# A fused attention-plus-MLP block: the opening's transposes as a stream of their own, V in column halves, small zero products

## The chip, the cores and the metric

The kernel runs on one core of one Trainium2 chip. The time is that of one execution on the device, in microseconds; the time before is the median of 6 runs. The engines are TensorE (PE; its weight loads are PEld), VectorE (DVE), ScalarE (ACT), GpSimd (POOL) and SyncE (SP), which issues the DMAs.

## The reference

Inputs are bf16: tokens x of 2048 x 640, `wqkv` 640 x 1920, 32 small matrices `w_phi` of 20 x 20, `wo` 640 x 640, `w1` and `w3` 640 x 1536, `w2` 1536 x 640.

```python
xn = layernorm(x)                                   # over 640
q, k, v = split(xn @ wqkv)                          # 32 heads of 20
pq, pk = q @ w_phi, k @ w_phi                       # per head
phi_q = concat(softmax(pq), softmax(-pq))           # 40 features per head
phi_k = concat(softmax(pk), softmax(-pk))
kv, z = phi_k^T @ v, sum(phi_k)                     # over 2048 tokens
o = (phi_q @ kv) / (phi_q . z + 1e-6)
out = x + o @ wo + (silu(xn @ w1) * (xn @ w3)) @ w2
```

## The kernel before

There are 16 token tiles of 128 rows, and 4 blocks of 512 tokens. `x_tok` holds the tokens, `xnT` the normalised tokens transposed (640 features as 5 chunks of 128 partitions). PSUM has 8 banks; a step asks `banks(1)` or `banks(2)` for the bank or pair that comes free first.

The work is written as Python generators, *streams*, that yield steps; a step is a short function which issues a few instructions on any of the engines. A planner in the kernel's own Python puts the steps in order: it keeps a clock for each engine, gives each instruction a planned cost, and at every turn takes the step whose planned start is earliest; between equals, the stream with the lower number goes first. A step with TensorE work can't be planned to start before TensorE is free plus 0.15; a step without any that belongs to a stream in `URGENT` is taken ahead when its engine will reach it within 4 planned microseconds of TensorE's clock. MLP steps go last while VectorE's clock is more than `LAG` = 4.0 ahead of TensorE's. The order of each engine's queue is fixed by that when the program is built; on the chip the engines wait for each other by semaphores.

The streams before are, in order of number:

- `norms`: the first loads and constants (`first_loads`, `consts`), then for each tile the statistics (`ln_stats`: VectorE, and POOL for the reciprocal root) and the normalisation in place (`ln_apply`); then `block_diag` on POOL, the later tiles, and at the end `consts_late`, which writes `eps` and the column of ones of `v2` on POOL.
- `fold_k`: five steps that fold w_phi into the K weights, giving `Wkp`, from `wqkT`, which a DMA transposes.
- `attention`: zero products, the transposes and V of tiles 0 to 3, then K (`k_tile`, two exponentials on ACT into `ekt`) and V (`v_tile`) of the other tiles with the Q fold (`Wqp`), then the sum over tokens (`kv_sum`, `kv_store`), then Q (`q_proj`, `q_tok`).
- `k_norms`: the softmax sums of K on VectorE (`S64`, `rS64`) and the division on POOL.
- `loads`: for tiles 4 to 15 the DMA transposes of normalised tokens into `xnT`, with the rest of the weight loads between them on SP's queue.
- `o_transposes`, `mlps` (48 steps of 10 products of 512 columns, with a tanh on ACT and two operations on VectorE), and `outs` (the output products of each tile, after the MLP).

The first four tiles are transposed on TensorE: `xn_transpose` makes five transposes into a bank of PSUM, and `evac` copies the bank to `xnT` on ACT or VectorE, whichever is planned to be done first. `v_tile` makes ten products of 320 columns into two banks, and ACT copies them into `v2`. In `attention` the order of these steps is written out by hand:

```python
yield lambda: warm_up(10, True)
yield from transposed(0)
yield lambda: warm_up(4, False)
yield from transposed(1)
yield v(0)
yield from transposed(2)
yield v(1)
yield from transposed(3)
yield v(2)
yield v(3)
```

`transposed(t)` yields nothing until `ln_apply(t)` is planned. `warm_up(n, first)` clears 512 columns of the tile `t1` and multiplies them n times; nothing reads the result, in bank 7.

Of the kernel before, what the change touches and what calls it, by code (L numbers as in the profile page):

```python
# [3 lines left out]
ACT = mybir.ActivationFunctionType  # L4
# [7 lines left out]
DH = 20  # L12
F = 1536
T = S // 128
DC = D // 128
# [227 lines left out]
def bass_parallel_sum__linear_kernel_hedgehog__glu_gated_swiglu__prompt_kernel(  # L243
# [48 lines left out]
    xnT = new("xnT", [128, DC, S], bf)  # L292
# [14 lines left out]
    wv = new("wv", [128, DC, D], bf, RKV + 6400)  # L307
# [14 lines left out]
    v2 = new("v2", [128, T, H * 21], bf, RV)  # L322
# [16 lines left out]
    def bank(k, cols=512, off=0, rows=128):  # L339
        return PS[0:rows, k * 512 + off:k * 512 + off + cols]  # L340
# [5 lines left out]
    def mm(o, l, r, start, stop, shared=False, cost=None):  # L346
        n = free(r)
        P.op("PE", "matmul", [o], [l, r], (o, l, r),
             dict(start=start, stop=stop, skip_group_check=shared),
             cost=max(n / 2400 + 0.003, 0.055) if cost is None else cost)  # L350
# [5 lines left out]
    def free(ap):  # L356
        n = 1
        for s in ap.shape[1:]:
            n *= s
        return n  # L360

    def act(o, i, f, scale=1.0):
        P.op("ACT", "activation", [o], [i], (o, i, f), dict(scale=scale),
             cost=0.17 + free(o) / 1200)
# [21 lines left out]
    def memset(eng, o, v):  # L386
        P.op(eng, "memset", [o], [], (o, v), cost=0.15 + free(o) / 960)
# [18 lines left out]
    def load_x(a, b):  # L406
        P.dma("SP", x_tok[:, a:b, :], x_t[:, a:b, :])
# [53 lines left out]
            P.op("ACT", "activation", [o], [o, s, z], (o, o, ACT.Identity), dict(bias=z, scale=s),  # L461
                 cost=0.9)

    def warm_up(n, first):

        z = t1[:, 2, :]
        if first:
            memset("DVE", z, 0.0)
        for _ in range(n):
            mm(bank(7), z[:, 0:128], z, True, True)  # L470

    def xn_transpose(t, k):
        for dc in range(DC):
# [29 lines left out]
    def proj(t, w, k):  # L503
        for q in range(2):
            for i in range(DC):
                mm(bank(k + q, 320), xnT[:, i, t * 128:(t + 1) * 128],
                   w[:, i, 320 * q:320 * q + 320], i == 0, i == DC - 1)

    def v_tile(t, k):
        proj(t, wv, k)  # L510
# [158 lines left out]
    def banks(n):  # L669

        def free_at(k):
            return max([o.end for i in range(k, k + n) for o in P.bank.get(("P", i), {}).values()],
                       default=0.0)
        return min(range(0, 8, n), key=free_at)

    done = dict.fromkeys(("w", "ln", "t", "f", "k", "n", "kv", "q", "o", "h"), 0)

    def norms():
        yield lambda: (first_loads(), consts())
        for t in range(4):  # L680
            yield lambda t=t: ln_stats(t, 1)
            if t:
                yield lambda t=t: ln_apply(t - 1)
                done["ln"] = t
        yield lambda: ln_apply(3)
        done["ln"] = 4
        yield block_diag
        todo = []
        for t in range(4, T + 2, 2):
            if t == T or t > done["k"] + 8 or t == 12 and done["w"] < 8:  # L690
                for u in todo:
                    yield lambda u=u: ln_apply(u)
                    done["ln"] = u + 1
                todo = []
            if t == T:
                break
            while t > done["k"] + 8 or t == 12 and done["w"] < 8:
                yield None
            yield lambda t=t: ln_stats(t, 2)
            for u in todo:  # L700
                yield lambda u=u: ln_apply(u)
                done["ln"] = u + 1
            todo = [t, t + 1]
        yield consts_late

    def fold_k():
        for dc in range(DC):
            yield lambda dc=dc: fold_mm(1, dc, banks(2))
        done["f"] += 1
# [3 lines left out]
    def k_norms():  # L713
        for t in range(T):
            while done["k"] <= t:
                yield None
            yield lambda t=t: k_norm(t)
            done["n"] = t + 1

    def transposed(t):  # L720
        while done["ln"] <= t:
            yield None
        yield lambda: xn_transpose(t, banks(1))
        done["t"] = t + 1

    def loads():
        while done["t"] < 4:
            yield None
        for t in range(4, T):
            while done["ln"] <= t:  # L730
                yield None
            yield lambda t=t: P.dma("SP", xnT[:, :, t * 128:(t + 1) * 128], x_tok[:, t, :], True)
            done["t"] = t + 1
            if t == 7:
                yield lambda: (w13(512, 1024), load_x(12, 16))
                done["w"] = 8
            if t == 9:
                yield lambda: w13(1024, 1536)
                done["w"] = 12
                yield lambda: P.dma("SP", wqkT[:, 0:DC, :], A_wqkv[:, 0:D], True)  # L740
                done["f"] = 2

    def attention():
        def v(t):
            return lambda: v_tile(t, banks(2))

        yield lambda: warm_up(10, True)
        yield from transposed(0)
        yield lambda: warm_up(4, False)
        yield from transposed(1)  # L750
        yield v(0)
        yield from transposed(2)
        yield v(1)
        yield from transposed(3)
        yield v(2)
        yield v(3)
        while done["f"] < 1:
            yield None
        for t in range(T):
            while done["t"] <= t:  # L760
                yield None
            yield lambda t=t: k_tile(t, banks(2))
            done["k"] = t + 1
            if t >= 4:
                yield v(t)
            if 9 <= t < 14:
                while done["f"] < 2:
                    yield None
                yield lambda dc=t - 9: fold_mm(0, dc, banks(2))
        yield lambda: P.dma("SP", wo_s[:], A_wo.rearrange("(c p) d -> p c d", p=128))  # L770
        for fc in range(DC):
            yield lambda fc=fc: q_proj(0, fc, banks(1))
        while done["n"] < T:
            yield None
        yield lambda: memset("POOL", stg[:], 0.0)
        yield lambda: kv_sum((0, 1, 2, 3), banks(1))
        yield lambda: kv_sum((4, 5), banks(1))
        yield lambda: kv_store((0, 1, 2), banks(1))
        yield lambda: kv_store((3, 4), banks(1))
        done["kv"] = 1  # L780
        yield lambda: P.dma("SP", w2_s[:], B_w2.rearrange("(c p) d -> p c d", p=128))
        yield lambda: (load_xres(0), load_xres(1))
        for b in range(NB):
            for j in range(4):
                t = 4 * b + j
                yield lambda t=t: q_tok(t, 0)
                done["q"] = t + 1
                if b + 1 < NB:
                    for fc in range((5 * j + 3) // 4, (5 * j + 8) // 4):
                        yield lambda b=b, fc=fc: q_proj(b + 1, fc, banks(1))  # L790

    def o_transposes():
        for t in range(T):
            while done["q"] <= t:
                yield None
            yield lambda t=t: P.dma("SP", oT[:, :, t * 128:(t + 1) * 128], o_tok[:, t % 3, :], True)
            done["o"] = t + 1

    def mlps():
        for b in range(NB):  # L800
            for fc in range(FC):
                while done["t"] < 4 * b + 4 or done["w"] <= fc or b == 2 and done["t"] < T or b == 3 and not done["kv"]:
                    yield None
                yield lambda b=b, fc=fc: mlp(b, fc, banks(2))
            done["h"] = b + 1

    def outs():
        for t in range(T):
            while done["o"] <= t or done["h"] <= t // 4:
                yield None  # L810
            yield lambda t=t: out_tile(t, banks(2))

    MLPS = 6
    URGENT = {0: 4.0, 3: 4.0}
    streams = [norms(), fold_k(), attention(), k_norms(), loads(), o_transposes(), mlps(), outs()]
    n = len(streams)
    heads, alive = [None] * n, [True] * n
    while any(alive):
        best = None
        for i in range(n):  # L820
# [14 lines left out]
            if any(o.eng == "PE" for o in ops):  # L835
                at = max(P.ready(ops), P.free["PE"] + 0.15)
                if i == MLPS and P.free["DVE"] > P.free["PE"] + LAG:
                    rank = n
            else:
                at = P.start_of(ops[0])  # L840
                if i in URGENT:
                    now, mine = P.free["PE"], P.free[ops[0].eng]
                    if at <= max(now, mine) + 0.3 and at < now + URGENT[i]:
                        at = now + 0.1 - URGENT[i]
            if best is None or (round(at, 2), rank) < best[:2]:
# [3 lines left out]
        i, ops, after = best[2:]  # L849
# [65 lines left out]
```

The softmax here doesn't subtract the row's maximum and nothing guards it: scores larger than these inputs give would overflow.

## Time and profile before

| what | value |
|---|---|
| median of 6 runs | 277.71 us (277.48 to 278.0) |
| the profiled execution: time, span | 278.18 us, 276.5 us |
| TensorE busy | 268.9 us (97% of the span) |
| VectorE, ScalarE, GpSimd busy | 182.1, 106.3, 60.3 us |
| HBM read, written | 12.81 MB, 2.62 MB |
| TensorE clock granted, as recorded | 1.00 |

The span runs from the first to the last instruction. A row of a timeline has the start, the length, the engine, the line, the operation, what it writes and reads, and how many equal instructions it stands for; the idle time before it and what ended that stand in brackets. Nearly all instructions are recorded by one helper, so all rows show line 101, and one goes by the names of tiles. `PS` is PSUM, `t` is `t1`, `w_s` stands for the MLP's weights and `S`, `rS` for the softmax sums and their reciprocals. Matmuls are pipelined: a row's length includes the end of the last one, and the distance between the starts of rows is what one costs in a stream.

### The profile page before, as it was taken

What the parts mean: (1) busy time and instruction counts of PE and PEld (TensorE: products, weight loads), DVE (VectorE), ACT (ScalarE), POOL (GpSimd) and SP (SyncE); (2) the same over time, 40 slices, a digit from 0 to 9 for tenths busy, and PEclk for the clock granted to TensorE, in tenths of its full rate; (3) what the DMA queues carried; (4) which work ended last, traced back from release to release, by engine and by line L of the source; (5) the groups of instructions that cost most, each with busy time, mean ns of one, the idle gap of its engine ahead of it and who ended that gap; (6) DMA issues with size and microseconds to landing.
All of it is one profiled execution on the core that took longest, in us unless ns stands there. A gap on an engine that the chain in (4) does not pass through costs nothing.

```text
span 276.5 us, 4669 instructions
## 1 busy us (share of the span) xinstructions
PE 268.9 (97%) x1898; PEld 163.3 (59%) x1916; DVE 182.1 (66%) x319; ACT 106.3 (38%) x192; POOL 60.3 (22%) x93
## 2 busy tenths in 40 slices
PE   7899989999999999999999999999999999999996
PEld 2556666667448445555555555666446777777774
DVE  5459779898763897999899899978863111121212
ACT  2377978598922225444644545221220000000000
POOL 4415297899990100000000000000000000000000
PEclk9999999999999999999999999999999999999999
DMA  7971799630000810211111211322300222222211
GB/s 199 294 225 37 208 253 281 105 120 2 0 0 2 284 51 0 51 24 24 26 24 34 39 24 25 51 53 67 72 0 2 76 66 78 67 77 68 75 47 47
DMA packets 40326, 21.96 MB, mean 79 GB/s; under 512 B 26736, under 2 KB 40304, under 8 KB 40304
## 3 DMA queue, kind: packets, MB, share of 16 engines
q1 hardware_dynamic: 40304, 21.66, 30.9%
q8 instruction: 15, 0.25, 0.4%
q14 instruction: 7, 0.06, 0.1%
HBM read 12.81 MB, written 2.62 MB: 56 GB/s over the span
## 4 chain that ended last, share of the span: by engine, by line
PE 78%; DVE 6%; SPq 5%; DMA 5%; POOL 3%; issue 1%; ACT 0%; POOLq 0%; ACTq 0%
PE PS L101 78%; SPq L113 5%; DMA x_tok<-in_A_x_dram 5%; DVE bst L101 4%; POOL ekt L101 2%; POOL v L101 1%; DVE mv L101 1%; DVE S L101 1%; POOL eps L101 0%; ACT v L101 0%; DVE hT L101 0%; DVE t L101 0%; ACT Wqp L101 0%; DVE rS L101 0%; DVE xres L101 0%
## 5 line engine op out<-in xcount | busy, mean ns | idle before, releaser
L101 PE MATMUL PS<-xnT,w_s 128*128 128x512 bf16 x467 | 105.4, 379 | 0.7
L101 PEld LDWEIGHTS PS<-xnT,w_s 128*128 128x128 bf16 x480 | 46.7, 98 | 55.2 <-ACT Wkp L101 0.2
L101 PE MATMUL PS<-w_s,hT 128*128 128x320 bf16 (+2 forms) x384 | 54.9, 299 | 0.0
L101 DVE TENSOR_TENSOR xres<-PS,xres 128x640 bf16<-128x640 f32 (+2 forms) x17 | 13.3, 785 | 54.0 <-PE PS L101 54.0
L101 ACT ACTIVATE th<-PS 128x512 f32<-128x512 f32 x48 | 28.6, 599 | 46.0 <-PE PS L101 46.0
L101 PEld LDWEIGHTS PS<-w_s,hT 128*128 128x128 bf16 x384 | 37.6, 98 | 14.6
L101 DVE SCALAR_TENSOR_TENSOR t<-th,PS 128x512 bf16<-128x512 f32 x48 | 32.8, 683 | 16.6 <-ACT th L101 16.6
L101 POOL TENSOR_TENSOR ekt<-ekt,rS 128x640 bf16<-128x640 bf16 x32 | 39.5, 1277 | 4.1 <-DVE rS L101 4.1
L101 DVE SCALAR_TENSOR_TENSOR hT<-t,PS 128x512 bf16<-128x512 bf16 x48 | 33.0, 687 | 1.8 <-PE PS L101 0.2
L101 ACT ACTIVATE EqT<-PS 128x512 bf16<-128x512 f32 x40 | 21.7, 594 | 9.9 <-PE PS L101 9.9
L101 PE MATMUL PS<-Wkp,xnT 128*128 128x320 bf16 x160 | 23.9, 299 | 0.8 <-DMA xnT<-x_tok 0.7
L101 PE MATMUL PS<-wo_s,oT 128*128 128x320 bf16 (+2 forms) x160 | 24.5, 299 | 0.0
L101 DVE TENSOR_TENSOR prod<-PS,g_s 128x1280 bf16<-128x1280 f32 x16 | 23.9, 1491 | 0.6
L101 PE MATMUL PS<-wv,xnT 128*128 128x320 bf16 x160 | 24.2, 299 | 0.0
L101 ACT ACTIVATE ekt<-PS 128x640 bf16<-128x640 f32 x32 | 20.7, 719 | 6.1 <-PE PS L101 6.0
L101 DVE TENSOR_REDUCE S<-ekt 128x64 f32<-128x1280 bf16 x16 | 23.0, 1438 | 0.0
L101 PE MATMUL PS<-xnT,Wqp 128*128 128x512 bf16 x95 | 22.6, 379 | 0.3
L101 PEld LDWEIGHTS PS<-Wkp,xnT 128*128 128x128 bf16 x160 | 15.3, 98 | 7.2 <-ACT ekt L101 1.0
L101 PEld LDWEIGHTS PS<-wo_s,oT 128*128 128x128 bf16 x160 | 15.6, 98 | 6.1
L101 PEld LDWEIGHTS PS<-wv,xnT 128*128 128x128 bf16 x160 | 15.5, 98 | 5.9
L101 DVE BATCH_NORM_STATS2 bst<-x_tok 128x6 f32<-128x320 bf16 x32 | 15.3, 478 | 5.0 <-DMA x_tok<-in_A_x_dram 4.4
L101 ACT ACTIVATE e_s<-PS 128x64 f32<-128x64 f32 x32 | 9.0, 283 | 22.0 <-PE PS L101 21.0
(52 smaller groups left out, 161.0 us busy)
## 6 DMA issues: line engine op xcount, KB each, us to landing
w_s<-in_B_w_dram SPq DMA_DIRECT2D x6, 640.0 KB, 6.5
xres<-in_A_x_dram SPq DMA_DIRECT2D x16, 160.0 KB, 2.4
out_dram<-xres SPq DMA_DIRECT2D x15, 160.0 KB, 1.8
x_tok<-in_A_x_dram SPq DMA_DIRECT2D x3, 640.0 KB, 6.0
w_s<-in_B_w_dram SPq DMA_DIRECT2D x1, 1920.0 KB, 9.2
wv<-in_A_wqkv_dram SPq DMA_DIRECT2D x2, 400.0 KB, 4.7
wo_s<-in_A_wo_dram SPq DMA_DIRECT2D x1, 800.0 KB, 4.7
x_tok<-in_A_x_dram SPq DMA_DIRECT2D x4, 160.0 KB, 2.7
```

What stands on the lines that cost most here:

```text
L101: o = _Op(eng, lambda: m(*args, **kw), r, w, cost)
L113: o = _Op(eng, lambda: m(out, in_), self.regions(in_), self.regions(out), nbytes, True)
```

## The change

- The transposes of tiles 0 to 3 become a stream, `transposes`, which stands second, ahead of `fold_k`. So the planner decides where each goes. All later streams move up by one number, and `MLPS` and `URGENT` follow.
- V of tiles 0 to 3 is issued by column halves, `v_half(t, q)`: five products of 320 columns in one bank, and a copy of 320 columns on ACT. Each half is a step. Tiles 4 to 15 keep `v_tile`.
- The zero products before the first transposes are 7 of 512 columns instead of 10; then 10 rounds of 2 products of 88 columns, each over 64 of the 128 rows, and 8 rounds of 4 products of 66 columns, each over 32 rows. Products of one round write to different banks (0 to 3). The 4 zero products after tile 0 are gone.

```diff
-    def warm_up(n, first):
+    def warm_up():
 
         z = t1[:, 2, :]
-        if first:
-            memset("DVE", z, 0.0)
-        for _ in range(n):
+        memset("DVE", z, 0.0)
+        for _ in range(7):
             mm(bank(7), z[:, 0:128], z, True, True)
+        for n, cols, rep in ((2, 88, 10), (4, 66, 8)):
+            r = 128 // n
+            for _ in range(rep):
+                for i in range(n):
+                    mm(bank(i, cols), z[r * i:r * i + r, 0:128], z[r * i:r * i + r, 0:cols], True, True,
+                       cost=0.05 / n)
...
+    def v_half(t, q, k):
+        for i in range(DC):
+            mm(bank(k, 320), xnT[:, i, t * 128:(t + 1) * 128], wv[:, i, 320 * q:320 * q + 320],
+               i == 0, i == DC - 1)
+        act(v2[:, t, 336 * q:336 * q + 336].rearrange("p (h c) -> p h c", c=21)[:, :, 0:DH],
+            bank(k, 320).rearrange("p (h c) -> p h c", c=DH), ACT.Copy)
...
+    def transposes():
+        for t in range(4):
+            yield from transposed(t)
...
-        yield lambda: warm_up(10, True)
-        yield from transposed(0)
-        yield lambda: warm_up(4, False)
-        yield from transposed(1)
-        yield v(0)
-        yield from transposed(2)
-        yield v(1)
-        yield from transposed(3)
-        yield v(2)
-        yield v(3)
+        yield warm_up
+        for t in range(4):
+            while done["t"] <= t:
+                yield None
+            for q in range(2):
+                yield lambda t=t, q=q: v_half(t, q, banks(1))
...
-    MLPS = 6
-    URGENT = {0: 4.0, 3: 4.0}
-    streams = [norms(), fold_k(), attention(), k_norms(), loads(), o_transposes(), mlps(), outs()]
+    MLPS = 7
+    URGENT = {0: 4.0, 4: 4.0}
+    streams = [norms(), transposes(), fold_k(), attention(), k_norms(), loads(), o_transposes(), mlps(), outs()]
```

## The prediction

> **What bounds the kernel now.** The page first: TensorE is busy for nearly the whole span, and the chain that ended last is TensorE for 78%, the rest being a load and normalisation chain early on.
>
> ```profile
> PE 268.9 (97%) x1898; PEld 163.3 (59%) x1916; DVE 182.1 (66%) x319; ACT 106.3 (38%) x192; POOL 60.3 (22%) x93
> ...
> PE 78%; DVE 6%; SPq 5%; DMA 5%; POOL 3%; issue 1%; ACT 0%; POOLq 0%; ACTq 0%
> ```
>
> So time is TensorE's work plus its idle time. 276.5 - 268.9 = 7.6 us idle. The waits of TensorE say where its larger holes are (the rest is the tail, where the last output leaves):
>
> ```profile
> PE PS L101 <- DVE x_tok L101: 1.6, 3, 0.9
> PE PS L101 <- DVE t L101: 1.3, 1, 1.3
> PE PS L101 <- DMA xnT<-x_tok: 0.7, 1, 0.7
> PE PS L101 <- ACT v L101: 0.3, 1, 0.3
> ```
>
> The timeline of TensorE gives each its place (start, length, instruction, idle before it):
>
> ```profile
> 1.29 4.08 PE L101 MATMUL PS<-t 128*128 128x512 bf16 x10 [1.29 <-DVE t L101]
> 5.94 0.45 PE L101 MATMUL PS<-ident,x_tok 128*128 128x128 bf16 x5 [0.57 <-DVE x_tok L101]
> 6.23 1.03 PE L101 MATMUL PS<-t 128*128 128x512 bf16 x4
> 7.42 0.45 PE L101 MATMUL PS<-ident,x_tok 128*128 128x128 bf16 x5 [0.17 <-DVE x_tok L101]
> 7.71 1.52 PE L101 MATMUL PS<-wv,xnT 128*128 128x320 bf16 x10
> 10.13 0.45 PE L101 MATMUL PS<-ident,x_tok 128*128 128x128 bf16 x5 [0.90 <-DVE x_tok L101]
> 10.42 1.52 PE L101 MATMUL PS<-wv,xnT 128*128 128x320 bf16 x10
> 11.78 0.44 PE L101 MATMUL PS<-ident,x_tok 128*128 128x128 bf16 x5
> 12.06 2.88 PE L101 MATMUL PS<-wv,xnT 128*128 128x320 bf16 x20
> ...
> 40.29 1.52 PE L101 MATMUL PS<-Wkp,xnT 128*128 128x320 bf16 x10 [0.70 <-DMA xnT<-x_tok]
> ...
> 56.59 0.49 PE L101 MATMUL PS<-BDc,wqkT 128*128 128x140 bf16 x6 [0.32 <-ACT v L101]
> ```
>
> From starts: a V half (5 matmuls of 320 columns) takes (11.78 - 10.42)/2 = 0.68, five transposes 6.23 - 5.94 = 0.29. The opening ends when V of tile 3 has issued, 12.06 + 4 x 0.68 = 14.78. In it TensorE stands without work from 9.07 to 10.13, because the hand-written order puts the transposes of tile 2 ahead of V of tile 1, and these wait for VectorE, which had waited for the loads. V of tile 1 could have run: its transposed tokens left PSUM by 8.62 (ACT, 7.92 + 0.70).
>
> **Zero products.** Seven of 512 columns instead of ten, the four later ones gone, and 52 small ones added. The ten start about 0.43 apart (4.08 for ten), the four 0.22, so the first run at half rate; seven end issuing at 1.29 + 7 x 0.43 = 4.28. The 52 must fit before the transposes of tile 0, ready at 5.94. No row shows a product in a row tile. The nearest is the KV sum, small products in column tiles, 4.96 us for 176, 28 ns each; 52 x 28 = 1.46. A change of tile mode shows there as about 0.10 (expected next start 84.44 + 2 x 0.216 = 84.87, found 84.97), and there are three: 4.28 + 1.46 + 0.30 = 6.04, 0.10 past 5.94. The upper row is the transposes, 56 ns each with full 128-column weights: 52 x 56 + 0.30 = 3.2, ending at 7.49; at half rate twice that, ending at 10.4. Below nothing is excluded: the removed products end no wait. I take the KV row, because the weight loads themselves seem cheap with 128 columns:
>
> ```profile
> L101 PEld LDWEIGHTS PS<-ekt,v 128*63 128x63 bf16 x160 | 4.2, 110 | 0.4 <-issue 0.4
> ...
> L101 PEld LDWEIGHTS PS<-ident,x_tok 128*128 128x128 bf16 x20 | 1.2, 98 | 3.1 <-DVE x_tok L101 3.0
> ```
>
> A load of 128 columns is recorded shorter (98 ns) than one of 63 (110 ns). The Trainium skill, "TensorE: Matmul & The Clock Gate", section "LDWEIGHTS (loading the stationary operand)", speaks against the change: a load costs its columns over 1.2 GHz whatever its rows, 107 ns for 128, so cutting the rows saves nothing and 52 loads would be an estimated 5.5 us, the transposes of tile 0 starting near 10. The row is far below the rule: five such loads start within 0.29 us.
>
> **Transposes as a stream, V by halves.** No product is added: 20 transposes and 40 matmuls as before. Walking the new order with the durations above:
> - Transposes 0 at 5.94 to 6.23, evicted by ACT until 7.13 as now; V0 first half 7.18 to 7.86 (with the four products gone, 1 us idle lies ahead of it).
> - Transposes 1 to 8.15, V0 second half to 8.83. ACT evicts 1 behind V0's copy, to about 9.2; V1 first half 9.25 to 9.93.
> - Transposes 2 remain bound by VectorE: 10.13 to 10.42. V1 second half to 11.10; tile 2 is evicted at 11.11 as now; V2 first half 11.16 to 11.84; transposes 3 (ready 11.47) to 12.13; then three halves, the last ending at 14.21 with 0.04 lost on an eviction.
>
> Gain 14.78 - 14.21 = **0.57**. From tile 0 alone the list needs 7.93 us, ending at 13.87, so a late tile 0 is free up to 0.34 and costs the whole gain at 0.91. If the planner puts transposes 1 ahead of V0, nothing changes: tiles 2 and 3 set the end.
>
> ACT copies V in eight pieces of 320 columns for four of 640. By ACT's rows (640: 0.71, 64: 0.28) one of 320 is about 0.47, so 4 x (2 x 0.47 - 0.71) = 0.9 us more, on an engine busy for 3.55 of the 9.0 us from 6 to 15; eight PSUM banks hold the halves. Uncovered, it would cost at most the last copy's 0.47. First MLP products follow at once: their weights left the queue before w_phi, which POOL used at 12.58.
>
> **What happens to 0.57 later.** SP's queue and the loads don't move: the wqkT transpose issues from 6.40 to 13.27 and tokens of tiles 4-7 land at 18.22, whatever TensorE does. So a lead can be lost where TensorE next meets that chain, at 40.29, where K of tile 8 waits 0.70 for its transposed tokens. The planner builds the order from its own due times. Followed by hand as a rule of order (its costs are not used as times), it meets this point with TensorE free earlier than the transfer by more than its margin, and then puts an MLP chunk (10 products of 0.216, 2.16 us) ahead of K of tile 8 instead of waiting. That work has to be done anyway, so the 0.70 vanishes. Likewise the third Wkp copy moves to VectorE (about 0.8 us, where VectorE is idle before 18.22), which costs nothing. The wait of 0.32 at 56.59 hangs on ACT's copy behind POOL's memset of v2; I leave it in the sum, since its place in POOL's queue may move either way (0.32 gained, or rival three). From 57.18 on TensorE has work without a hole, so a lead there reaches the end.
>
> Sum: 0.57 + 0.70 = 1.27 off. The profiled execution took 278.18 (span 276.5 and 1.68 around it), 0.47 above the median 277.71; taken off the median: 277.71 - 1.27 = 276.44, say **276.4**. Both edges: 0.3 more from 56.59 and up to 0.2 from small waits, 275.9; half of the 0.70 regained by new short waits, 276.9.
>
> **Rivals.**
> - The lead is eaten: order as before, and TensorE waits at 40.29 for 1.27 instead of 0.70, or later. For it: that wait is on a DMA chain rooted in SP. Against: the planner fills such holes with MLP work. Nothing left is 277.7; only 0.57 left, 277.1. Chance 0.21.
> - Slower: the small products overrun. Place: ahead of transposes 0. At 56 ns each they end at 7.49, tile 0 is 1.55 late, less the 0.34 free: 1.21 - 0.57 = 0.64 slower, 278.3; at half rate 3.5 slower, about 281. It decides from 42 ns each on ((5.94 + 0.91 - 4.58)/52 = 44, less a little for the switches' spread). Less zero work could also leave TensorE at half rate when V starts: each half would cost 0.68 more. For it: no row of this form; against: 28 ns and 98 ns above. Chance 0.14.
> - Slower: the MLP chunk's two VectorE operations (0.68 + 0.69) go ahead of a K normalisation, POOL's chain and the v2 memset end 1.3 later, and ACT's V copy holds the PSUM banks at 56.59 that much longer: 277.7 + 1.3 = 279.0. For it: VectorE is busy 10.85 of 12 us from 45 to 57. Against: by the same rule the memset may fall behind that V copy, which then doesn't wait. Chance 0.10.
>
> The first case keeps 0.55. What can be told from no change is 0.2%, 0.56 us: faster below 277.15. Faster: 0.55 and 0.08 of the first rival, 0.63; same: the rest of it, and 0.01 of the second, 0.14; slower: 0.13 + 0.10 = 0.23. The range runs from 275.9 to 278.3; outside lie the third rival, half-rate products, and a few in a hundred below.
>
> **What would show it.** After: 7 long zero products, then 52 ending before about 6.2; the transposes of tile 0 near 5.94 and those of tile 2 near 10.13 with V halves on both sides; last V product issued near 14.2, against 14.78; no DMA wait at K of tile 8, with an MLP chunk ahead of it; TensorE's busy time down by about 0.5 to 1.5 and no new wait over 0.5 before 60 us. I am wrong if transposes 0 start past 6.85, if V starts at twice 0.136 a product, or if idle time past 15 us grows.

## The result, and the profile after

The changed kernel takes 276.81 us in the median of 17 runs (276.2 to 277.88), the kernel before 277.86 beside it (37 runs): 1.05 us less, ratio 0.996 with an interval of 0.9948 to 0.9973. The forecast was 276.4, faster, with a range of 275.9 to 278.3. The sum came out; two of its terms did not.

The profiled execution took 277.25 (span 275.5; before 276.5). Its page, busy time and chain:

```profile
PE 269.8 (98%) x1942; PEld 164.7 (60%) x1961; DVE 181.9 (66%) x318; ACT 108.2 (39%) x197; POOL 60.8 (22%) x93
...
PE 96%; DVE 1%; DMA 1%; issue 0%; ACT 0%
```

The chain is now TensorE from start to end (96%, before 78%): the load and normalisation chain that had held it up until 57 us is gone. TensorE's waits say the same. Four became two, and neither of those left lies behind the opening:

```profile
PE PS L101 <- DVE t L101: 1.3, 1, 1.3
PE PS L101 <- ACT xnT L101: 0.8, 1, 0.8
```

But busy time rose, from 268.9 to 269.8, where it should have fallen by 0.5 to 1.5. The timeline of TensorE in the opening shows why:

```profile
1.29 4.58 PE L101 MATMUL PS<-t 128*128 128x512 bf16 x59 [1.29 <-DVE t L101]
5.95 0.71 PE L101 MATMUL PS<-ident,x_tok 128*128 128x128 bf16 x5
7.46 1.52 PE L101 MATMUL PS<-wv,xnT 128*128 128x320 bf16 x5 [0.80 <-ACT xnT L101]
8.77 0.74 PE L101 MATMUL PS<-ident,x_tok 128*128 128x128 bf16 x5
9.30 2.20 PE L101 MATMUL PS<-wv,xnT 128*128 128x320 bf16 x10
11.34 0.44 PE L101 MATMUL PS<-ident,x_tok 128*128 128x128 bf16 x5
11.62 1.60 PE L101 MATMUL PS<-wv,xnT 128*128 128x320 bf16 x10
13.06 0.44 PE L101 MATMUL PS<-ident,x_tok 128*128 128x128 bf16 x5
13.34 2.28 PE L101 MATMUL PS<-wv,xnT 128*128 128x320 bf16 x15
```

The order is the one that was listed. But five transposes take 0.71 where they took 0.45, and half of V of tile 0 1.31 from start to start (8.77 - 7.46) where 0.68 was counted: TensorE ran at half rate until about 10.7. V of tile 3 was done issuing at 15.45 (the first MLP product seen starts at 15.67; one record of 0.22 ahead of it is missing). Before, it was 14.78. This execution lost 0.67 in its opening and still ended sooner.

Behind the opening, the same view where K of tile 8 waited before (start 40.29, wait 0.70) and where the third Q fold did (start 56.59, wait 0.32):

```profile
40.33 2.11 PE L101 MATMUL PS<-xnT,w_s 128*128 128x512 bf16 x9
42.27 1.52 PE L101 MATMUL PS<-Wkp,xnT 128*128 128x320 bf16 x10
...
55.94 0.48 PE L101 MATMUL PS<-BDc,wqkT 128*128 128x140 bf16 x6
56.26 1.52 PE L101 MATMUL PS<-Wkp,xnT 128*128 128x320 bf16 x10
```

An MLP chunk stands ahead of K of tile 8, and no bracket with a wait is left. By starts: V of tile 7 to the first Q fold holds the same work (one of its two MLP chunks now stands earlier) and went from 11.97 (38.07 to 50.04) to 11.11 (38.75 to 49.86), 0.86; from there to the third Q fold 6.55 became 6.08, 0.47; from that to K of tile 12, 0.59 became 0.32, 0.27. That is 1.60 gained, less 0.67 lost: 0.93 of the span's 1.0.

The third Q fold no longer waits because POOL's order changed. Before, and then after (the first 12 of 26 divisions in a row, and the write behind them):

```profile
53.36 2.37 POOL L101 MEMSET v<- 128x512 bf16 x1
```

```profile
48.31 14.78 POOL L101 TENSOR_TENSOR ekt<-ekt,rS 128x640 bf16<-128x640 bf16 x12 [1.64 <-DVE rS L101]
82.21 2.37 POOL L101 MEMSET v<- 128x512 bf16 x1
```

The write of ones into `v2` now comes behind the K divisions of all 16 tiles instead of 5, so ACT's V copies no longer wait for it.

### The profile page after: what moved, and what is told of

Its sections match the earlier page's. It is cut to its first block, busy times and chain, and to the rows that moved or that the text cites. A ratio compares the mean times of both kernels' runs of the same rounds, so it can differ in the third digit from the quotient of the medians.

```text
span 275.5 us, 4763 instructions
## 1 busy us (share of the span) xinstructions
PE 269.8 (98%) x1942; PEld 164.7 (60%) x1961; DVE 181.9 (66%) x318; ACT 108.2 (39%) x197; POOL 60.8 (22%) x93
## 4 chain that ended last, share of the span: by engine, by line
PE 96%; DVE 1%; DMA 1%; issue 0%; ACT 0%
PE PS L101 96%; DMA x_tok<-in_A_x_dram 1%; DVE bst L101 1%; ACT xnT L101 0%; DVE xres L101 0%; DVE mv L101 0%; DVE x_tok L101 0%
## 5 line engine op out<-in xcount | busy, mean ns | idle before, releaser
L101 PE MATMUL PS<-wv,xnT 128*128 128x320 bf16 x160 | 25.9, 310 | 0.8 <-ACT xnT L101 0.8
```

Of the source, the lines that this page charges most:

```text
L101: o = _Op(eng, lambda: m(*args, **kw), r, w, cost)
```

## The experiments

Two questions were left. For the lost rate (the first four experiments), theory 1 blames the small products in row tiles, that is, over a part of the 128 rows, and theory 2 the idle time where the four products were; "dense" products are those over all 128 rows. For the gain (the next three), theory 1 puts it into the order behind the opening, the opening itself being worth little here; each names its rival. "Before" and "after" are short for the two kernels. Each kernel was timed beside the kernel before; differences are taken between medians of one job.

### Ten dense zero products in the kernel after

```diff
-        for _ in range(7):  ... 7 products of 512 columns, then 20 of 88 and 32 of 66
+        for n in range(10):
+            mm(bank(7), z[:, 0:128], z, True, True, cost=0.2414)
```

> The kernel after, with ten zero products of 512 columns ahead of tile 0 in place of seven and the 52 small ones; their planned cost is the same sum, so the order of all else stays (one MLP chunk later on changes places with a Q step). Theory 1, the small products in row tiles don't bring TensorE to full rate, the dense ones do: V of tile 0 starts at 0.136 a product instead of 0.267, the opening ends near 14.2 instead of 15.46, and the time falls to about 275.6 to 275.9, with less spread from run to run. Theory 2, the rate is lost in the idle time behind tile 0's transposes, where the four products were: V still starts at half rate and the time stays near 276.8.

Measured 276.17 (276.01 to 276.78, 6 runs) beside 277.74: -1.57, ratio 0.9947 (0.9931 to 0.9963). In its profile TensorE is still at half rate at 5.96 (five transposes 0.71) but at full rate from 7.46 on, and the opening ends at 14.39. It goes with theory 1 in direction; the time is 0.3 above what that expected.

### The four products put back into the kernel after

```diff
+        if t == 0:
+            for _ in range(4):
+                mm(bank(3), z[:, 0:128], z, True, True, cost=0.0)
```

> The kernel after, with the four zero products of 512 columns put back behind tile 0's transposes, at no planned cost, so the order of all else is that of after. Theory 1 (the row tiles): TensorE is still at half rate there, the four take 1.7 us instead of 0.86, V of tile 0 starts near 8.2 instead of 7.46; time 276.8 to 277.4. Theory 2 (the idle time): full rate soon after the four, V at 0.136 a product, opening ends near 14.6; time near 276.0.

Measured 277.21 (276.63 to 277.86, 12 runs) beside 277.74: -0.53, ratio 0.9981 (0.9971 to 0.9991), so no better than after. Theory 1 had the time right, but the profile, one of its quickest executions (276.73), shows neither theory's opening: zero products done after 4.15, full rate from 5.95, opening ended at 13.98. Even so little of that lead is kept: the fold of w_phi, the next step behind one MLP chunk, waits 0.33 for the transposed `wqkT` and starts at 16.63. What the slower executions lose is in no profile.

### The small zero products in the kernel before

```diff
-        for _ in range(n):
+        for _ in range(7 if first else n):
             mm(bank(7), z[:, 0:128], z, True, True)
+        ... the 52 small ones, if first
```

> The kernel before, with its ten zero products replaced by the seven and the 52 small ones of after (planned sum unchanged, so the same order); the four behind tile 0 stay. Theory 1: transposes and the first V products run at half rate; the opening ends 0.5 to 1.2 us later than 14.78, and as the order still waits at K of tile 8 (0.86 by starts), most of the loss is absorbed there: 277.7 to 278.3, with more spread. Theory 2: as before, 277.8.

Measured 278.14 (277.6 to 278.9, 12 runs) beside 277.74: +0.40, ratio 1.0013 (1.0003 to 1.0024). The time is as theory 1 expected; theory 2 would have it unchanged. The reason that theory 1 gave is not seen: it had the opening end 0.5 to 1.2 later than 14.78, and in the profile (278.0) only the transposes of tile 0 run slowly (0.67) and the opening ends at 14.58.

### The kernel before without the four

```diff
-        yield lambda: warm_up(4, False)
```

> The kernel before without the four zero products behind tile 0's transposes; the order of all else is unchanged. Theory 1 (the row tiles lose the rate): ten dense products are enough, nothing in the opening moves, since transposes 1 wait for VectorE: 277.8. Theory 2 (the four keep the rate): V of tile 0 at half rate, opening later by 0.5 to 1 us, absorbed in part at K of tile 8: 277.9 to 278.5.

Measured 278.28 (277.89 to 279.17, 12 runs) beside 277.74: +0.54, ratio 1.0024 (1.0013 to 1.0036). Theory 1 said no change, so it does not hold alone: the row tiles and the missing four both cost something. But the one profile (279.09) has full rate from 7.33 on. Its later end sits in transfers that landed later, K of tile 8 above all:

```profile
PE PS L101 <- DMA xnT<-x_tok: 1.4, 1, 1.4
```

What the four do in the median is therefore not read from a trace.

### Only the order: one chunk ahead of K of tile 8, in the kernel before

```diff
+            while t == 8 and nmlp[0] < 4:
+                yield None
             yield lambda t=t: k_tile(t, banks(2))
```

> The kernel before, whole opening unchanged, with one edit: K of tile 8 may not be planned until four MLP chunks are. The planner then also puts the writing of eps and of the ones of v2 on POOL behind the K divisions, as in after; from the first MLP chunk on the order is that of after but for one chunk. Theory 1 (the gain of after lies in the order behind the opening, the opening itself loses some of it): the three waits of before go, 0.86 by starts at K of tile 8, 0.47 at the third Q fold and 0.27 behind it, 1.60 in all: about 276.1, below after's 276.8. Rival (the earlier end of the opening pays): without it the chunk only fills a hole and the chain from SP holds TensorE up later; 277.1 or more.

Measured 276.58 (276.44 to 277.32, 6 runs) beside 277.87: -1.29, ratio 0.996 (0.9945 to 0.9975). The planner then also puts the write of ones behind the divisions of all 16 tiles. With the old opening entire, this is the gain of after, though 0.5 slower than the 276.1 expected. TensorE's waits behind the opening are gone:

```profile
PE PS L101 <- DVE x_tok L101: 1.8, 3, 1.0
PE PS L101 <- DVE t L101: 1.3, 1, 1.3
```

What is left are the holes of the old opening. The rival (277.1 or more) falls.

### Only the write of ones, moved behind

```diff
+        while done["n"] < 13:
+            yield None
         yield consts_late
```

> The kernel before, with only the writing of eps and of the ones of v2 moved behind the K divisions of 13 tiles on POOL; the MLP chunk stays where it was. Theory 1: the wait on ACT's V copy at the third Q fold goes with what follows it, 0.47 + 0.27 = 0.74 less, about 277.0, and the DMA wait at K of tile 8 stays. Rival: the copies were held by something else too, and TensorE waits there all the same: 277.5 to 277.8.

The planner then put it behind all 16, POOL's order in after. Measured 276.90 (276.71 to 277.33, 8 runs) beside 277.87: -0.97, ratio 0.9971 (0.9959 to 0.9982). The wait at the third Q fold is gone, and the DMA wait at K of tile 8 is there still, at 0.21 in this profile, since that transfer landed sooner (K starts at 39.70). Expected was -0.74.

### The kernel after with the chunk held behind K of tile 9

```diff
-  ... or b == 3 and not done["kv"]:
+  ... or b == 3 and not done["kv"] or b == 0 and fc == 3 and done["k"] < 10:
```

> The kernel after, but the fourth MLP chunk may not be planned before K of tile 9 is, as it was in the order of before; eps and the ones of v2 stay late. Theory 1: the DMA wait at K of tile 8 is back, some 0.9 us, longer where the opening ends early, so the opening hardly shows in the time: 277.0 to 277.7. Rival (the opening's own lead carries through): 276.8 or below, as after.

Measured 277.65 (277.16 to 278.6, 12 runs) beside 277.87: -0.22, ratio 0.9994 (0.9982 to 1.0007). The chunk's place is thus worth 0.83 of after's 1.05 (277.65 against 276.81 in other jobs, -0.22 against -1.05 beside before). The profile has the wait back, 0.68 at 40.69, and one more far ahead of it, at the first fold product:

```profile
PE PS L101 <- DMA wqkT<-in_A_wqkv_dram: 0.8, 1, 0.8
PE PS L101 <- DMA xnT<-x_tok: 0.7, 1, 0.7
...
17.36 1.76 PE L101 MATMUL PS<-BDc,wqkT 128*128 128x140 bf16 x30 [0.83 <-DMA wqkT<-in_A_wqkv_dram]
```

That second wait is seen only in kernels with the small zero products (0.34 in the second profile of after, 0.33 with the four put back). From issue to landing the transposed `wqkT` took 8.9 in the profile of before and 10.3 in that of after:

```profile
DMA to landing us min/median/max: 8.9/8.9/8.9
```

```profile
DMA to landing us min/median/max: 10.3/10.3/10.3
```

Over all fourteen profiles it is 10.2 to 10.7 in the six with small zero products and 8.6 to 9.6 in the eight without. Why is shown by no run. Behind the opening TensorE and POOL have the same order here as with only the write of ones moved (276.90 in the same job), while on ACT and VectorE some copies and normalisations stand elsewhere; with the changed opening this kernel is 0.75 slower.

Its opening is instruction for instruction that of after, and in this execution TensorE had its full rate from 7.40:

```profile
5.95 0.65 PE L101 MATMUL PS<-ident,x_tok 128*128 128x128 bf16 x5
7.40 0.85 PE L101 MATMUL PS<-wv,xnT 128*128 128x320 bf16 x5 [0.80 <-ACT xnT L101]
8.09 0.44 PE L101 MATMUL PS<-ident,x_tok 128*128 128x128 bf16 x5
```

It ends at 14.20; the list in the prediction said 14.21. Same instructions, 14.20 here and 15.45 in the profile of after: what differs is when TensorE reaches its full rate. Yet the fold starts at 17.36 here and at 17.61 there, so most of the 1.25 is gone by then.

### Dense products and the four, in the kernel after

The edits of the first two experiments together.

> The kernel after with ten dense zero products ahead of tile 0 and the four behind its transposes, the order of all else that of e1. If the rate is still half there, the four cost 1.7 and V of tile 0 starts near 8.2, else 0.86 and V starts on time. Theory 1 (the full rate comes at a moment that differs from run to run, and more zero work only makes it likelier): near e1, 276.0 to 276.6. Rival (the four are what secures the rate): clearly below e1, 275.7.

Measured 275.96 (275.72 to 276.56, 6 runs) beside 277.87: -1.91, ratio 0.9936 (0.9922 to 0.9951), the fastest of all. In its profile the rate is full from 5.89 and the opening ends at 13.91. Its fold starts at 16.08 without a wait. Beside the order alone, in the same job, the opening is worth 0.62. The time lies between theory 1 (276.0 to 276.6) and its rival (275.7), so it decides nothing between these two.

### Three of them on one chip

> The kernel after itself, on the same chip as the next three. Its opening was seen to end at 15.46 in one profile and at 14.20 in another (of the kernel with the chunk behind), so its times should spread by more than 1 us, and a new profile may show either: 276.5 to 277.2 in the median.

> The dense zero products and the four, beside after on one chip. Theory: the opening as streams and halves is worth the 0.57 that its list says, once TensorE runs at full rate; so 0.6 below the kernel before with the chunk ahead, and 0.6 to 1.1 below after: about 276.0. Rival (the differences between chips made it): the same as these two within 0.2.

> The kernel before with the chunk ahead of K of tile 8, beside the others on one chip. Theory: the order behind the opening is all of after's gain, so no slower than after: 276.5. Rival (the opening of after gains as well): slower than after by 0.3 or more.

Measured beside 278.00: after 276.84 (276.72 to 277.24, 6 runs), ratio 0.9961 (0.9947 to 0.9976); dense and four 276.43 (276.03 to 276.87, 6 runs), 0.9947 (0.993 to 0.9965); order alone 276.96 (276.48 to 277.51, 9 runs), 0.9959 (0.9946 to 0.9972). After and the order alone can't be told apart (0.12). Dense and four lies 0.53 below the order alone, as it lay 0.62 below in the job before, and 0.41 below after, where 0.6 to 1.1 was expected. The intervals of the ratios overlap, so the size rests on two jobs that agree, not on one that decides. Against what was expected, after did not spread by 1 us in these 6 runs (0.5), while it did over the 17 above (1.7). Its new profile has full rate from 5.82, and its opening ends at 14.42.

### Zero products in row tiles alone

```diff
+        for _ in range(80):
+            for i in range(4):
+                mm(bank(i, 66), z[32 * i:32 * i + 32, 0:128], z[32 * i:32 * i + 32, 0:66], True, True,
+                   cost=2.414 / 320)
```

> The kernel after with zero products in row tiles alone: 80 rounds of four of 66 columns over 32 rows, of about the same length in time (80 x 0.055 = 4.4 at half rate), planned sum and order unchanged. Theory (products in row tiles count less towards the full rate than products over all rows): zero products and V of tiles 0 and 1 at half rate in the profile, and slower than after, 277.2 to 278. Rival (they count alike, and only the moment differs from run to run): as after.

Measured 280.21 (279.16 to 280.64, 6 runs) beside 278.00: +2.21, ratio 1.0075 (1.0057 to 1.0094). It does not answer its question. TensorE stood still in the middle:

```profile
1.29 3.26 PE L101 MATMUL PS<-t 32*128 32x66 bf16 x223 [1.29 <-DVE t L101]
6.91 0.96 PE L101 MATMUL PS<-t 32*128 32x66 bf16 x97 [2.36 <-issue]
```

The hole of 2.36 waits for nothing that the profile shows, tile 0 starts 1.85 late for it (7.80), and V of tile 0 then runs at half rate. Whether products over part of the rows count less towards the full rate stays open.

## Why the prediction was right or wrong

**The opening, 0.57.** The list of steps held where TensorE had its rate in time: 14.20 measured (the experiment with the chunk behind), 14.21 predicted. With dense products and the four the opening is worth 0.62 and 0.53 of the time. In the kernel as changed it is worth nothing that can be told: 0.12 between after and the order alone on one chip, and a loss of 0.75 with the chunk held behind. Two steps failed.

The first: all of the list's durations were taken at full rate from tile 0 on. "Less zero work could also leave TensorE at half rate when V starts" stood as a side remark in the second rival, without a price in the sum. The profile of after lost 0.67 to it.

The second: "SP's queue and the loads don't move", so that a lead would next meet that chain at 40.29. It met it at the fold. Before, `wqkT` had landed at 15.30 (6.40 + 8.9), 1.64 ahead of the fold at 16.94; in the five profiles with the 7 and the 52 products it landed between 16.5 and 17.2. Nor does SP's queue go on regardless of TensorE: in all fourteen profiles the first transpose of tokens issued 7.72 or 7.73 after the first fold product (16.94 and 24.66 before, 16.08 and 23.80 with dense and four).

Three profiles of this opening end at 15.45, 14.42 and 14.20, 14.69 in the mean; four of the old one with its own zero products (before, the order alone twice, the write of ones alone) at 14.78, 14.49, 15.03 and 14.68, 14.75 in the mean. By the start of the fold it is 17.61, 17.09 and 17.36 against 16.94, 16.65, 17.19 and 16.83, so 0.45 later in the mean. The term is about zero at the end of the opening and less than that at the fold. The changed zero products are what eats it, as the dense ones in their place show; the two ways are seen in profiles, their shares in the median are not known.

**The fit of the 52 products.** Right: they had to end before 5.94, the KV row gave 6.04, and the last of their loads ended at 5.71. The row that decided it, 98 ns for a load of 128 columns against 110 for one of 63, pointed the right way, but it compares recorded lengths, and what a load costs in a stream is the distance between starts. The loads of the row tiles after:

```profile
4.39 1.32 PEld L101 LDWEIGHTS PS<-t 64*128 64x128 bf16 x52 [0.84 <-issue]
```

52 loads in 1.32, 25 ns each, at half rate; 0.80, 15 ns each, in the second profile of after. The rule weighed there, 107 ns for 128 columns ("TensorE: Matmul & The Clock Gate", section "LDWEIGHTS (loading the stationary operand)"), is near the recorded length of one load (97 and 93 ns over 64 and 32 rows in that second profile), but as a price per load it is four to seven times too much here, since the loads overlap. The second rival's mechanism, an overrun ahead of tile 0, did not happen.

**The wait at K of tile 8, 0.70.** Right in mechanism and place: the planner put an MLP chunk there, and holding that chunk back costs 0.83. The wait was taken from the bracket, which counts from the modelled end of the last product; by starts the hole is 0.86. Nor is it the same in every execution: with only the write of ones moved the bracket says 0.21. The first rival's outcome is what that experiment shows, -0.22 without the chunk, but not at its place: TensorE waits 0.68 at K of tile 8, not 1.27, and had lost 0.83 at the fold before.

**The wait at the third Q fold, left out of the sum.** This is the other mis-sized term. The text said that it may fall either way; it fell towards a gain, for the reason given against rival three, that the write of ones goes behind that V copy. Alone it is worth 0.97. The bracket said 0.32; by starts, with the K tile that also waited behind it, it was 0.47 + 0.27 = 0.74.

**The sum.** Predicted 0.57 + 0.70 + 0; found about 0 or less for the opening and 1.04 to 1.29 for the order, which is the median's 1.05 already. That 276.4 came so near to 276.81 is luck: an overcounted opening and an undercounted order nearly cancel. The two waits don't add in full either: the write of ones alone gave 0.97, both 1.29 in the same job and 1.04 in the next; the 0.83 for the chunk was measured with the changed opening. A slip that changes nothing: half of 0.70 on top of 276.44 is 276.8, not 276.9.

**The signs named beforehand.** Tile 0 at 5.95, an MLP chunk ahead of K of tile 8 and no new wait over 0.5 before 60 us apart from the 0.8 for the transposed tokens in the opening, listed there as 1 us idle, were all seen. TensorE's busy time fell in no way, and V at twice 0.136 a product was the named sign of being wrong: it is in the profile of after, for the opening.

## What to carry to other kernels

A change at the start of a queue-ordered program is worth what the next waits let through: look for the waits behind it (here the fold at 17 us and K of tile 8 at 40 us), and ask whether work can be put in front of them; one line that did only that gained as much as this change. Don't take the end of such a wait as fixed: in the five profiles that wait there, K of tile 8 starts anywhere from 39.70 to 41.22. Take the size of a hole from start to start at known cost per instruction, not from the idle time in the bracket. And price the rate at which TensorE starts as a term of the sum: what is taken out of a warm-up, or put into it in another form, can be paid for in executions that one profile does not show.

## What the runs showed of the hardware

- Equal instruction streams reach full rate at different moments: ten dense zero products in the profiles took 3.66, 4.01, 4.08, 4.44 or 4.45 us, and V of tile 0 ran at half rate until 10.7 in one profile of after and at full rate from 7.07 in another. The Trainium skill, "TensorE: Matmul & The Clock Gate", section "The HAM clock gate" (Part 1), has a window of about 3.4 us that runs free of the program; the profiles agree in that the moment varies, and no run here shows the window itself.
- The granted clock in the profile does not show this: it stands at 1.00 through the half-rate start of after. In the kernel with row tiles alone it shows 0.82 for 6 to 10 us.
- Four products of 66 columns in four row tiles ran at 14 ns each (224 loads in 3.11). In the one profile of that kernel TensorE stood 2.36 us after 223 such products, waiting for nothing that the profile shows.
- With small zero products over part of the rows the transposed `wqkT` landed 10.2 to 10.7 us after its issue (six profiles), without them 8.6 to 9.6 (eight). The cause is open.
